# Clustered attention and a gated FFN on one core: one pair of heads turned by DMA in place of TensorE, and the next pair's turns put behind it

## The chip, the cores and the metric

The kernel runs on one core of a Trainium2 chip. The metric is the device time of one execution in microseconds (us); a lower one is better. The profiles are of single executions, taken by the hardware profiler.

## What is computed

Four batches of eight heads, 768 tokens, 64 numbers per head. Each query and key is assigned to one of 16 clusters (the centroid with the largest product); a query attends to the keys of its own cluster alone. The attention's result, heads side by side, goes through an FFN with a sigmoid gate.

```python
q_assign = argmax(q_n @ c_n.T); k_assign = argmax(k_n @ c_n.T)
mask   = q_assign[:, :, :, None] == k_assign[:, :, None, :]
scores = where(mask, scale * q @ k.T, -1e9)
attn   = softmax(scores)
x      = (attn @ v) as [4 * 768, 512]
out    = (sigmoid(x @ w_gate) * (x @ w_val)) @ w_out      # 512 -> 1536 -> 512
```

## The kernel before

**Heads as tiles.** For each head there is a tile `T` of 128 partitions by 12 blocks of 128 columns: six blocks of keys, six of queries, with the 64 numbers in partitions 0 to 63 and tokens along the columns. It comes from `hl`, the same with tokens in partitions: the numbers in f16 ("hi", a cast) and their rounding errors ("lo", a subtraction). Turning `hl` gives `T`. One group of 12 small matmuls per head then gives the cluster logits `lg`; VectorE takes their largest and writes one-hot rows `oh`, which are turned in their own right and laid over partitions 64 to 79 of `T` (in the queries as a large negative number where the cluster differs). One matmul of `T`'s keys against its queries then gives masked scores.

**Steps.** Everything runs to a clock of steps. A step is one scores matmul (line 1066: one block of keys against 384 queries), its exponential on ScalarE (line 1071), and the products of an earlier step with the values (line 1089). Batch 0 has steps 0 to 95, batch 1 steps 96 to 191, and so on. Pairs of heads are numbered 0 to 3; in batch 1 pair 0 is used from step 96 (its second head from 108), pair 1 from 120, pair 2 from 144. Between these, in each step, a queue of FFN work of the batch before is let out by a credit in nanoseconds: gate groups (`g`, line 532) and value groups (`v`, line 548) of four matmuls, then output products (`o`, line 865).

**The order of work** on each engine is the order in which the program emits it, and each engine works in order. What prepares a later pair is put at a step by a number in the table `SCHED`; half a step means ahead of the step's FFN work, a whole one behind it. The numbers `b1p1...` count from the step at which the pair is used; those of `g0...` and `g1...` are steps themselves.

**Two ways to prepare a pair.** `pieces` (batch 1's first `npe` pairs) turns on TensorE: six transposes at a time into a PSUM tile (line 1198), eviction by VectorE or ScalarE (lines 1211, 1209), the one-hot rows likewise (line 1250, then 1261 and 1263). Its steps are `hi`, `lo`, `tu`, `ev`, `lg`, `pk`, `ot`, `pl`. `pair_prep` (all other pairs of batches 1 to 3) turns by DMA from SyncE's queue: `sp` (cast on VectorE, line 1631, and subtraction on GpSimd, line 1632, for keys or queries of one head), `tn` (one DMA that turns a head, line 412), `lg` and `pk` (logits; their reading, the choice and the one-hot rows, lines 436, 451 to 471), `ot` (one DMA that turns a pair's one-hot rows, line 1649), `hp` (two small DMAs per head that carry them into `T`, line 492, here called hops).

```python
def turn(key, hl, pl):
    T[key] = pl.tile([128, hl.shape[1], 128], HP, tag="T", name="T")
    SP.dma_start_transpose(out=T[key], in_=hl.rearrange("p c x -> p (c x)"))
...
NPE = SCHED.get("npe", 1)
PEP = [(1, p) for p in range(NPE)]
...
for e in range(0 if (b, p) in PEP else 2):     # in pair_prep: nothing of a pair that pieces prepares
```

On SyncE's queue stand besides these the loads of later pairs (line 213), the stores of the result (line 504), and the turns of attention results `x` by DMA (line 1120; of batch 0's second half, those of pairs 1 and 2, at steps 74 and 87; the product that they wait for is GpSimd's, line 390). PSUM has four banks in a ring for scores, gates, values and logits, two for the value products, and two for outputs and for what TensorE transposes.

Of the kernel before, what the change touches and what calls it, by code (L numbers as in the profile page):

```python
# [19 lines left out]
]  # L20
SCHED = {
# [74 lines left out]
    "fwv": [354, 356, 357, 359, 364, 366, 370, 371], "b3p2pk1": -28.5, "END": 0,  # L96
}


# [1671 lines left out]
```

## Time and profile before

| | us |
|---|---|
| median of 3 runs | 318.93 (318.47 to 319.13) |
| the profiled execution | 319.12 |
| its span in the profile | 317.3 |
| TensorE busy | 310.0 |
| ScalarE busy | 244.9 |
| VectorE busy | 238.6 |
| GpSimd busy | 120.9 |

The span runs from the first instruction's start to the last one's end; what lies outside it is start and end of the program. A row of the timeline gives start, duration, engine, line, operation, what is written and read, and how many instructions it stands for. Matmuls overlap: a row's duration includes the tail of its last one, so the time that a group takes up is read from its start to the next row's start. For DMAs the duration is that of the issue on the queue; the landing is told apart.

### The profile page before, as it was taken

What the parts mean: (1) busy time and instruction counts of PE and PEld (TensorE: products, weight loads), DVE (VectorE), ACT (ScalarE), POOL (GpSimd) and SP (SyncE); (2) the same over time, 40 slices, a digit from 0 to 9 for tenths busy, and PEclk for the clock granted to TensorE, in tenths of its full rate; (3) what the DMA queues carried; (4) which work ended last, traced back from release to release, by engine and by line L of the source; (5) the groups of instructions that cost most, each with busy time, mean ns of one, the idle gap of its engine ahead of it and who ended that gap; (6) DMA issues with size and microseconds to landing.
All of it is one profiled execution on the core that took longest, in us unless ns stands there. A gap on an engine that the chain in (4) does not pass through costs nothing.

```text
span 317.3 us, 9228 instructions
## 1 busy us (share of the span) xinstructions
PE 310.0 (98%) x3492; PEld 218.8 (69%) x3492; DVE 238.6 (75%) x623; ACT 244.9 (77%) x555; POOL 120.9 (38%) x157
## 2 busy tenths in 40 slices
PE   7899999999999999999999999999999999999995
PEld 4688766766666666666777678766677678656685
DVE  5899756778688777686788688776888776678983
ACT  6688998797899887877776876777877887588621
POOL 5888454244434275423234333424212111026600
PEclk9999999999999999999999999999999999999999
DMA  7999998639848988976676455882506130300014
GB/s 196 379 259 169 271 164 143 176 83 264 242 100 163 204 221 136 199 217 161 106 193 153 151 118 134 248 153 53 112 2 76 55 27 14 145 1 3 0 35 165
DMA packets 77996, 45.16 MB, mean 142 GB/s; under 512 B 56896, under 2 KB 75520, under 8 KB 77952
## 3 DMA queue, kind: packets, MB, share of 16 engines
q1 hardware_dynamic: 73840, 39.66, 51.3%
q0 software_dynamic: 3680, 4.72, 9.1%
q8 instruction: 27, 0.44, 0.6%
q10 hardware_dynamic: 432, 0.20, 0.2%
q14 instruction: 17, 0.14, 0.1%
HBM read 28.34 MB, written 6.29 MB: 109 GB/s over the span
## 4 chain that ended last, share of the span: by engine, by line
PE 93%; DMA 2%; DVE 1%; POOL 1%; SPq 1%; issue 0%; ACT 0%; DVEq 0%
PE sc L1066 19%; PE g L532 15%; PE v L548 15%; PE av L1089 11%; PE o L994 9%; PE o L865 5%; PE lg L436 2%; PE o L699 2%; PE o_end L802 2%; PE av L699 2%; DMA kraw<-in_k_dram 2%; PE v L628 2%; PE y L699 2%; PE o L802 1%; PE av L802 1%; PE z L699 1%
## 5 line engine op out<-in xcount | busy, mean ns | idle before, releaser
L1071 ACT ACTIVATE es<-sc 128x384 f16<-128x384 f32 x384 | 174.1, 492 | 38.5 <-PE sc L1066 29.8
L1066 PE MATMUL sc<-T 128*128 128x384 f16 x384 | 117.3, 325 | 0.7 <-DVE T L1396 0.4
L1089 PEld LDWEIGHTS <-es 128*128 128x128 f16 x1152 | 81.3, 98 | 35.1 <-ACT es L1071 0.2
L1089 PE MATMUL av<-va,es 128*128 128x65 f16 x1152 | 97.6, 194 | 0.0
L553 DVE SCALAR_TENSOR_TENSOR hT<-th,v 128x384 f16<-128x384 f32 x72 | 39.8, 553 | 33.8 <-PE av L1089 29.6
L377 POOL TENSOR_TENSOR xp<-t,rec 128x384 f16<-128x384 f32 (+1 forms) x30 | 21.8, 726 | 97.3 <-DVE rec L374 49.2
L548 PE MATMUL v<-xTb,wv 128*128 128x384 f16 x288 | 58.5, 326 | 0.1
L532 PE MATMUL g<-xTb,wg 128*128 128x384 f16 x288 | 58.5, 326 | 0.0
L538 ACT ACTIVATE th<-g 128x384 f32<-128x384 f32 x72 | 35.4, 492 | 8.3 <-PE g L532 6.3
L1066 PEld LDWEIGHTS <-T 128*128 128x128 f16 x384 | 37.0, 96 | 1.2 <-DVE T L1396 0.7
L548 PEld LDWEIGHTS <-wv 128*128 128x128 f16 x288 | 28.0, 97 | 13.9 <-issue 0.3
L532 PEld LDWEIGHTS <-wg 128*128 128x128 f16 x288 | 27.9, 97 | 13.9
L1632 POOL TENSOR_TENSOR hl<-kraw,hl 128x384 f16<-128x384 f32 x22 | 20.2, 920 | 40.6 <-DVE hl L1631 25.9
L1632 POOL TENSOR_TENSOR hl<-qraw,hl 128x384 f16<-128x384 f32 x22 | 21.1, 961 | 11.1 <-DVE hl L1631 11.1
L865 PE MATMUL o<-wo,hT 128*128 128x512 f16 x72 | 19.9, 379 | 0.0
L372 DVE TENSOR_TENSOR t<-av,sv 128x390 f32<-128x390 f32 (+1 forms) x30 | 14.4, 480 | 7.1 <-PE av L1089 5.3
L941 DVE TENSOR_TENSOR ob<-o,ob 128x256 f32<-128x256 f32 (+1 forms) x28 | 15.0, 549 | 4.7 <-PE o L994 3.2
L708 POOL TENSOR_TENSOR hT<-T 128x384 f16<-128x384 f32 x12 | 11.8, 1001 | 16.2 <-DVE T L657 15.6
L994 PE MATMUL o<-wo,hT 128*128 128x256 f16 x108 | 16.8, 272 | 0.0
L994 PEld LDWEIGHTS <-sum 128*128 128x128 f16 x144 | 14.0, 97 | 3.3
L451 DVE TENSOR_REDUCE lgs<-lg 128x192 f32<-128x384 f32 x23 | 12.7, 551 | 3.0 <-PE lg L436 2.9
L324 POOL CAST va<-vraw 128x768 f16<-128x768 f32 x15 | 13.1, 873 | 2.4 <-DMA vraw<-in_v_dram 2.4
(225 smaller groups left out, 470.2 us busy)
## 6 DMA issues: line engine op xcount, KB each, us to landing
vraw<-in_v_dram SPq DMA_DIRECT2D x15, 384.0 KB, 4.9
kraw<-in_k_dram SPq DMA_DIRECT2D x14, 384.0 KB, 4.2
qraw<-in_q_dram SPq DMA_DIRECT2D x12, 384.0 KB, 4.1
out_dram<-ob SPq DMA_DIRECT2D x17, 256.0 KB, 2.2
wg<-in_moe_w_gate_dram POOLq DMA_DIRECT2D x2, 768.0 KB, 9.2
wv<-in_moe_w_val_dram POOLq DMA_DIRECT2D x2, 768.0 KB, 10.4
wo<-in_moe_w_out_dram POOLq DMA_DIRECT2D x2, 768.0 KB, 9.3
T<-ohT SPq DMA_DIRECT2D x44, 24.0 KB, 1.9
```

What stands on the lines that cost most here:

```text
L377: (eng or POOL).tensor_tensor(x, t[:, 0:nq, 0:64], bcast(rec[:, 0:nq], 64), ALU.mult)
L532: PE.matmul(out=g[:, 0:n], lhsT=wg[fc // WQ][:, dc, fc % WQ, :], rhs=xT[:, dc, t0 : t0 + n], start=(dc == 0), stop=(dc == NDC - 1),)
L538: ACT.activation(th[:, 0:n], g[:, 0:n], AF.Tanh)
L548: PE.matmul(out=w[:, 0:n], lhsT=wv[fc // WQ][:, dc, fc % WQ, :], rhs=xT[:, dc, t0 : t0 + n], start=(dc == 0), stop=(dc == NDC - 1),)
L553: DVE.scalar_tensor_tensor(HB[b, blk][:, fc, 0:n], st[0][:, 0:n], 1.0, w[:, 0:n], ALU.add, ALU.mult)
L699: PE.matmul(out=o, lhsT=l, rhs=r, start=start and d == 0, stop=stop and d == 1, skip_group_check=True,)
L865: PE.matmul(out=o, lhsT=HB[b, blk][:, fc, bass.ts(t, 128)], rhs=wo[fc // WON][:, fc % WON, :], start=(fc == 0), stop=(fc == NFC - 1),)
L994: PE.matmul(out=st[z][:, e], lhsT=a[:, c, :], rhs=rhs[:, c, :], start=start and c + e == 0, stop=c == HF - 1, skip_group_check=True,)
L1066: PE.matmul(out=sc.rearrange("p (c t) -> p c t", t=128), lhsT=s["k"], rhs=s["q"], start=True, stop=True,)
L1071: ACT.activation(es, sc, AF.Exp, scale=SCALE)
L1089: PE.matmul(out=av[:, a0 + s["c0"] + i, :], lhsT=s["es"][:, bass.ts(i, 128)], rhs=VA[b, p][:, e, s["j"], :], start=(first and i == 0 and a ...
L1632: POOL.tensor_tensor(hl[:, :, 64:128], r, hl[:, :, 0:64], ALU.subtract)
```

## The change

Three things are changed, all in the table `SCHED`. `npe` goes from 1 to 0, so that batch 1's pair 0 is prepared by `pair_prep` like the others: turned by two DMAs, its one-hot rows turned by a third and carried into `T` by four hops. Thirteen new numbers place its steps, counted from step 96 (`sp00` at -30 is step 66, `hp1` at -8 is step 88). And six numbers of pair 1, counted from step 120, are moved later: its casts and turns go from steps 60.5 to 79 to steps 71 to 80.

```diff
-    "halved1": 1, "halved0": 4, "npe": 1, ...
+    "halved1": 1, "halved0": 4, "npe": 0, ...
...
-    "b1p1sp00": -59.5, "b1p1sp01": -56.5, "b1p1tn0": -52, ...
-    "b1p1sp10": -48.5, "b1p1sp11": -46.5, "b1p1tn1": -41.0, ...
+    "b1p1sp00": -49, "b1p1sp01": -48, "b1p1tn0": -44, ...
+    "b1p1sp10": -45.5, "b1p1sp11": -44.5, "b1p1tn1": -40, ...
...
+    "b1p0sp00": -30, "b1p0sp01": -29, "b1p0sp10": -28, "b1p0sp11": -27,
+    "b1p0tn0": -25.5, "b1p0tn1": -23.5, "b1p0lg0": -17.5, "b1p0pk0": -16.5,
+    "b1p0lg1": -14.5, "b1p0pk1": -13.5, "b1p0ot": -12.5, "b1p0hp0": -8.5, "b1p0hp1": -8,
```

In steps, before and after:

| | before | after |
|---|---|---|
| pair 0, casts and subtractions | 68 to 85 | 66, 67 (head 0), 68, 69 (head 1) |
| pair 0, turns | 75.5, 78 (head 0), 84.5, 89.5 (head 1), on TensorE | 70.5, 72.5, by DMA |
| pair 0, logits | 79, 92 | 78.5, 81.5 |
| pair 0, one-hot rows turned | 82.5, 98.5, on TensorE | 83.5, by DMA |
| pair 0, one-hot rows placed | 83.5 to 104.5, by VectorE and ScalarE | 87.5, 88, by hops |
| pair 1, casts and subtractions | 60.5, 63.5, 71.5, 73.5 | 71, 72, 74.5, 75.5 |
| pair 1, turns by DMA | 68, 79 | 76, 80 |
| pair 1, logits | 81.5, 89 | 81.5, 89 |

More of the change, by code (lines that the diff above doesn't have):

```diff
@@ L95 @@
     "b3p0vs": -30, "b3p0vu": -28, "b3p0vt": -9, "b3p1lg0": -32, "b3p1pk0": -32, "fwg": [327, 327, 331, 331.5, 332, 341, 341, 344],
-    "fwv": [354, 356, 357, 359, 364, 366, 370, 371], "b3p2pk1": -28.5, "END": 0,
[1 row of a table added]
 }
```

7 rows, old and new, of the table SCHED are left out of this document.

## The prediction

> **What bounds the kernel now.** I read the page's busy times first, then its chain that ended last, then the busy times in the two stretches that the change touches.
>
> ```profile
> PE 310.0 (98%) x3492; PEld 218.8 (69%) x3492; DVE 238.6 (75%) x623; ACT 244.9 (77%) x555; POOL 120.9 (38%) x157
> ...
> PE 93%; DMA 2%; DVE 1%; POOL 1%; SPq 1%; issue 0%; ACT 0%; DVEq 0%
> ```
> ```profile
> 40.00:57.00 17.00, 17.00 (x177) 11.46 (x176) 10.74 (x28) 14.91 (x37) 9.28 (x12) 1.00 0.85 140
> 57.00:75.00 18.00, 18.00 (x217) 11.86 (x216) 13.14 (x35) 14.77 (x32) 5.11 (x7) 1.00 0.67 167
> ```
>
> The first pair of rows is the page's: TensorE (PE) is busy for 98% of the span and is 93% of the chain. The second pair gives stretch, length and busy time of PE, weight load, VectorE, ScalarE, GpSimd, then the granted clock (1.00), the DMA share and GB/s. PE is busy 17.00 of 17.00 us and 18.00 of 18.00 us, at full clock; VectorE has 6.3 us and 4.9 us to spare, GpSimd 7.7 us and 12.9 us, the DMA engines 15% and 33%. So a PE instruction taken out here is worth its slot, until PE has to wait for something; and a wait of PE costs its full length. I therefore read the PE timeline for the slots, and SyncE's (SP's) issues for the new waits.
>
> **What is removed.** Before, pair 0 of batch 1 is turned on PE, in four groups of six transposes for keys and queries (line 1198) and two of six for the one-hot rows (line 1250). Here are some groups, each with the row that follows it, and three logit groups and one score row that I use below:
>
> ```profile
> L1198 PE MATMUL t_ps<-identh,hl x24: 217/219/220, 55.2 to 68.2; 128*128 128x128 f16 x24
> ...
> L1250 PE MATMUL oh_ps<-identh,oh x12: 218/219/219, 61.7 to 75.5; 128*128 128x128 f16 x12
> ```
> ```profile
> 55.19 0.50 PE L1198 MATMUL t_ps<-identh,hl 128*128 128x128 f16 x6
> 55.52 0.81 PE L548 MATMUL v<-xTb,wv 128*128 128x384 f16 x4
> ...
> 58.83 0.45 PE L436 MATMUL lg<-cm,T 128*128 128x32 f16 x12
> 59.13 0.32 PE L1066 MATMUL sc<-T 128*128 128x384 f16 x1
> ...
> 61.10 0.45 PE L436 MATMUL lg<-cm,T 128*128 128x32 f16 x12
> 61.40 0.25 PE L1089 MATMUL av<-va,es 128*128 128x65 f16 x3
> ...
> 61.65 0.50 PE L1250 MATMUL oh_ps<-identh,oh 128*128 128x128 f16 x6
> 61.99 0.81 PE L532 MATMUL g<-xTb,wg 128*128 128x384 f16 x4
> ...
> 62.92 0.81 PE L548 MATMUL v<-xTb,wv 128*128 128x384 f16 x4
> 63.56 0.26 PE L1089 MATMUL av<-va,es 128*128 128x65 f16 x3
> 63.66 0.33 PE L1066 MATMUL sc<-T 128*128 128x384 f16 x1
> ...
> 67.44 0.45 PE L436 MATMUL lg<-cm,T 128*128 128x32 f16 x12
> ...
> 73.36 0.32 PE L1066 MATMUL sc<-T 128*128 128x384 f16 x1
> ```
>
> The 0.50 us of a group includes the tail of its last matmul; the slot is from its start to the next start: 55.52 - 55.19 = 0.33 us and 61.99 - 61.65 = 0.34 us, so 0.335 us for six, 56 ns each. Six groups are 6 x 0.335 = **2.0 us** of PE time, the whole possible gain. The logit groups (12 matmuls, 59.13 - 58.83 = 0.30 us each) stay two in number and only change place: head 0's stays at step 79, head 1's moves up from step 92 to just before pair 1's at step 82 (the row at 61.10).
>
> One rule speaks against taking this work off PE. The Trainium skill, "VectorE: DVE Perf Modes", sections "The three transpose paths" and "Rules for kernel authors", says to transpose 128x128 on TensorE where PSUM will do as destination and gives 390 ns for a block there against 1309 ns by DMA. By its figure, as an estimate, 36 blocks off PE would be 14 us; the slots above, in a stream that is never idle, say 2.0 us, and no run here shows a block in isolation. What the DMA path does here is worked out below from this trace's landings.
>
> Gone from ScalarE and VectorE are four evictions and four copies of one-hot rows, and VectorE gets two more casts and two small multiplications. Neither engine ends a wait of PE in these stretches, so I cost this at nothing: the cover is the idle time above, and GpSimd's extra subtractions (four in place of two and a cast) fit its 7.7 us.
>
> **What is added: DMA work on SP, and waits of PE for it.** These are SP's issues before, and for some of them the time from issue to landing (the view of DMA issues, cut to one issue at a time, in the order of the text).
>
> ```profile
> 50.19 1.44 SPq L412 DMA_TRANSPOSE T<-hl  x1
> 56.33 1.18 SPq L1120 DMA_TRANSPOSE xTb<-xp  x1
> 57.57 0.57 SPq L213 DMA_DIRECT2D kraw<-in_k_dram  x1
> 58.19 0.46 SPq L213 DMA_DIRECT2D vraw<-in_v_dram  x1
> 58.70 0.47 SPq L213 DMA_DIRECT2D qraw<-in_q_dram  x1
> 59.33 2.42 SPq L412 DMA_TRANSPOSE T<-hl  x1
> 67.91 1.18 SPq L1120 DMA_TRANSPOSE xTb<-xp  x1
> ...
> 72.22 1.21 SPq L1649 DMA_TRANSPOSE ohT<-oh  x1
> ...
> 77.37 2.50 SPq L492 DMA_DIRECT2D T<-ohT  x4
> ```
> ```profile
> T<-hl SPq DMA_TRANSPOSE x1, 3.3
> ```
> ```profile
> T<-hl SPq DMA_TRANSPOSE x1, 6.2
> ```
> ```profile
> ohT<-oh SPq DMA_TRANSPOSE x1, 5.1
> ```
> ```profile
> T<-ohT SPq DMA_DIRECT2D x1, 24.0 KB, 2.0
> ```
>
> (50.19, 59.33, 72.22, and the second of the four that begin at 77.37: at 0.6 us each it is issued at about 78.0.) The row at 50.19 is pair 1's first head (step 68), 59.33 its second (step 79). SP works in order, and so do the landings on its queue: 59.33 took 6.2 us because three loads of 384 KB went ahead. After, the order on SP is: pair 0's head 0 (step 70.5), its head 1 (72.5), the x turn of 56.33 (74), pair 1's head 0 (76), the three loads, pair 1's head 1 (80), pair 0's one-hot turn (83.5), the x turn of 67.91 (87), pair 0's four hops (87.5, 88). Everything that PE waits for there:
>
> ```profile
> 48.32 0.82 POOL L324 CAST va<-vraw 128x768 f16<-128x768 f32 x1
> 53.26 0.96 POOL L1632 TENSOR_TENSOR hl<-kraw,hl 128x384 f16<-128x384 f32 x1 [4.12 <-DVE hl L1631]
> 54.18 0.91 POOL L1632 TENSOR_TENSOR hl<-qraw,hl 128x384 f16<-128x384 f32 x1
> 55.48 0.82 POOL L390 TENSOR_TENSOR xp<-t,rec 128x384 f16<-128x384 f32 x1 [0.39 <-DVE rec L389]
> ```
>
> 1. Pair 0's turns. GpSimd's subtractions follow the cast of 48.32 and come 0.9 us apart, so two are ready at about 50.1 and four at 51.9 us. Head 0 is turned at 50.2 and lands 3.3 later, at 53.5; head 1 at 52.0 lands at 55.3. PE reads head 0 no earlier than 58.83 - 0.67 - 0.81 = 57.3 us (two groups gone, and a value group of 0.81 us that went ahead of it now behind it), head 1 at 61.10 - 0.67 = 60.4. Cover 3.8 and 5.1 us: no cost. Pair 1's first two subtractions end at about 53.7, ahead of the x product at 55.48, so the x turn stays at 56.33.
>
> 2. Pair 1's head 0 now stands behind that x turn: issue at 57.57, as kraw before, landing 3.3 later at 60.8 to 60.9. PE wants it at 61.10 - 0.67 + 0.30 (head 1's group ahead of it) = 60.7. Its cover was 61.10 - 53.5 = 7.6 us and is now nothing: a wait of 0.1 to 0.3 us.
>
> 3. Pair 1's head 1 stands behind the three loads, all later by one turn's issue, 1.44 us. Before it landed at 59.33 + 6.2 = 65.5; if it is later by that, 67.0; if the loads only close up behind the turn ahead of them, 66.2 (an estimate: half the delay). PE wants it at 67.44 - 4 x 0.335 + 0.30 = 66.4, or 66.6 with the wait of point 2: 0 to 0.4 us.
>
> 4. Two logit groups now lie side by side, in two of the four PSUM banks that scores, gates and values share, until VectorE has read both. One reading and choice takes
>
> ```profile
> 62.77 0.56 DVE L451 TENSOR_REDUCE lgs<-lg 128x192 f32<-128x384 f32 x1
> 63.36 0.35 DVE L462 TENSOR_REDUCE mx<-lgs 128x12 f32<-128x192 f32 x1
> 63.75 0.43 DVE L464 TENSOR_TENSOR oh<-lgs,mx 128x96 f16<-128x96 f32 x2
> 64.21 0.19 DVE L471 TENSOR_SCALAR oh<-oh 128x96 f16<-128x96 f16 x1
> ```
>
> that is 1.6 us; the first starts at about 61.0, so the second bank is read at 61.0 + 1.6 + 0.55 = 63.1. PE needs that bank again four or five allocations on, at the value group of 62.92 or the scores of 63.66, which after stand 0.67 + 0.34 - 0.30 = 0.7 us earlier and point 2's wait later, at 62.4 or 63.1: a wait of 0.7 us or of nothing. I take a quarter of a microsecond, since the wait of point 2 moves PE towards it.
>
> 5. Pair 0's hops, before head 0's scores at step 96 (73.36). One-hot turn at about 63.1 (SP is in the turn of point 3 until then). Before, from the one-hot turn's issue to the landing of the first head's second hop took 78.0 + 2.0 - 72.22 = 7.8 us; so 70.9. PE comes to step 96 at 73.36 - 5 x 0.335 = 71.7 plus the waits above. Cover 0.8 us or more: no cost.
>
> Sum: 2.0 - 0.2 - 0.15 - 0.25 = **1.4 us** gained. Nothing gives it back later: PE is the bound on both sides of these stretches. The profiled execution took 319.12 us (span 317.3 and 1.8 around it), so 317.7 for its like; it lies 0.2 us above the median of the runs, 318.93, so the forecast is **317.5 us**. With no waits it is 316.9; with all at their upper ends (0.3 + 0.4 + 0.7) it is 318.3.
>
> **The rivals.** A measurement of this kernel tells about 0.2%, 0.6 us, from no change.
>
> *The DMA queue eats the gain* (about the same time). The turn of point 3 grows: SP's descriptors back up one transfer earlier, its issue comes a microsecond later and it lands at 68.0 to 68.5; PE waits 1.5 us there, and 0.3 us before it: 318.7. For: the 2.42 us issue at 59.33, against 1.44 elsewhere, shows SP already held back behind three loads. Against: DMA engines are 33% idle there. Chance 0.15.
>
> *Head 0's one-hot rows come too late* (slower). On the DMA path the way from logits to placed rows crosses SP's queue twice, behind other transfers. It decides where the first head's second hop lands after 71.7 + 2.0 = 73.7 with no other wait, 10.6 us after the one-hot turn's issue; every microsecond beyond is lost. With a one-hot turn held 2 us by late choices on VectorE and a hop 2 us late behind the x turn of 67.91 (in front of the hops on SP), it lands at 75: 318.93 - 2.0 + 3.3 = 320.2. Against it: 7.8 us in the rows. Chance 0.13. The rule of the Trainium skill's page "VectorE: DVE Perf Modes" that is cited above would have this outcome, since it prefers TensorE wherever PSUM will do; the trace speaks for it only in the landing times, 3.3 to 6.2 us a turn.
>
> *The full 2.0 us* (no wait binds): 316.9. Part of the forecast's case below.
>
> **How the numbers follow.** Forecast case, gains from 0.7 to 2.0: 0.72. Queue case 0.15, slower case 0.13. Faster by over 0.2% takes the forecast case alone, 0.72; within 0.2% the queue case, 0.15; slower 0.13. The forecast's own range is 316.9 to 318.3. For 8 in 10 it takes in part of the queue case, up to 318.9, and 0.2 us of measurement below: 316.7 to 318.9.
>
> **What would show it.** Right: no groups at lines 1198 and 1250, PE 36 instructions fewer, turns from line 412 at 24 in place of 22 and hops at 48 in place of 44, with the first two turns near 50 and 52 us; small idle time of PE before logit groups around 60.5 and 66.5 us, under a microsecond in sum, and none at step 96; step 120 earlier by 1.2 to 2.0 us, and the end by as much. Wrong: a PE idle of over a microsecond before a logit group (queue case), or before the scores of step 96 released by the hops (slower case); a gain that is there at step 120 and gone at the end; or ends of waits on VectorE in many small pieces, which would mean that its slack was not there.

## The result

The changed kernel is slower: 320.76 us median (320.56 to 321.57) against 319.0 us for the kernel before, a ratio of 1.005 with a 95% interval of 1.0027 to 1.0074. Run again later with more executions the ratio was 1.0033 (1.0011 to 1.0055). The forecast was 317.5 us, between 316.7 and 318.9.

The profiled execution after took 321.57 us, with a span of 319.8 us; it is the slowest of the first four executions. Of its page, the busy times and the chain that ended last:

```profile
PE 309.1 (97%) x3456; PEld 217.3 (68%) x3456; DVE 238.4 (75%) x621; ACT 241.6 (76%) x550; POOL 122.3 (38%) x158
...
PE 82%; DMA 8%; DVE 4%; POOL 2%; issue 1%; ACT 1%; SPq 1%; DVEq 0%; POOLq 0%; ACTq 0%
```

TensorE has the 36 instructions fewer, but its share of the chain fell from 93% to 82%, and DMA and VectorE have taken that over. The view of waits, TensorE from 40 us on, names nobody before. After, it has three rows (who waited for whom, us in total, times, longest; `hT`, line 553, is the FFN's hidden product, which frees the PSUM bank of a value group):

```profile
PE lg L436 <- DMA T<-hl: 1.8, 2, 1.0
PE v L548 <- DVE oh L464: 1.0, 1, 1.0
PE lg L436 <- DVE hT L553: 0.5, 1, 0.5
```

On the timeline of TensorE these waits stand at four places, steps 79, 111, 116 and 130; the brackets give the idle time ahead and its releaser:

```profile
56.73 0.33 PE L1066 MATMUL sc<-T 128*128 128x384 f16 x1
57.59 0.28 PE L436 MATMUL lg<-cm,T 128*128 128x32 f16 x5 [0.53 <-DVE hT L553]
...
82.72 0.34 PE L548 MATMUL v<-xTb,wv 128*128 128x384 f16 x1 [1.01 <-DVE oh L464]
87.06 0.29 PE L436 MATMUL lg<-cm,T 128*128 128x32 f16 x5 [0.86 <-DMA T<-hl]
96.10 0.27 PE L436 MATMUL lg<-cm,T 128*128 128x32 f16 x4 [0.99 <-DMA T<-hl]
```

An idle time leaves out the tail of the matmul ahead. Measured from start to start, with the usual slot of the instruction ahead taken off, the four are 0.69, 1.17, 1.02 and 1.16 us; four smaller ones between steps 82 and 95 come to 0.76 and one at step 187 to 0.31. These nine sum to 5.1 us. Against the 2.0 us saved that makes 3.1 us lost. The scores rows of the two timelines come to 2.9: the lead-in, all that runs ahead of the change, happened to be 0.52 us shorter in the execution after, and from that

| step | start before | start after | after against before, lead-in taken off |
|---|---|---|---|
| 75 | 54.12 | 53.60 | 0.00 |
| 96 | 73.36 | 72.56 | -0.28 |
| 111 | 82.55 | 81.39 | -0.64 |
| 117 | 86.33 | 87.38 | +1.57 |
| 132 | 95.23 | 97.31 | +2.60 |
| 192 | 128.36 | 130.76 | +2.92 |
| 381 | 267.34 | 269.74 | +2.92 |

So there are two losses. Up to step 111 a gain of 2.0 us came to 0.64. Then, behind everything that the change adds, 3.6 us are lost, and afterwards nothing more. (The other three executions are 0.8 to 1.0 us shorter than the profiled one. A second profile, told below, lost less, and in part elsewhere.)

What stands behind the second loss is on SyncE's queue. First some rows of before: pair 2's two turns and pair 3's first (line 412), between them the loads of keys for pair 3 (73.49) and for a later pair (81.94). Then the queue after, from pair 0's one-hot turn on:

```profile
69.27 1.39 SPq L412 DMA_TRANSPOSE T<-hl  x1
...
73.49 0.57 SPq L213 DMA_DIRECT2D kraw<-in_k_dram  x1
...
79.92 1.35 SPq L412 DMA_TRANSPOSE T<-hl  x1
...
81.94 0.44 SPq L213 DMA_DIRECT2D kraw<-in_k_dram  x1
...
87.26 1.42 SPq L412 DMA_TRANSPOSE T<-hl  x1
```
```profile
62.92 2.54 SPq L1649 DMA_TRANSPOSE ohT<-oh  x1
66.96 1.18 SPq L1120 DMA_TRANSPOSE xTb<-xp  x1
69.88 2.49 SPq L492 DMA_DIRECT2D T<-ohT  x4
72.48 1.43 SPq L412 DMA_TRANSPOSE T<-hl  x1
...
75.11 1.23 SPq L1649 DMA_TRANSPOSE ohT<-oh  x1
76.39 0.57 SPq L213 DMA_DIRECT2D kraw<-in_k_dram  x1
...
80.80 2.44 SPq L492 DMA_DIRECT2D T<-ohT  x4
83.68 1.42 SPq L412 DMA_TRANSPOSE T<-hl  x1
...
85.78 0.44 SPq L213 DMA_DIRECT2D kraw<-in_k_dram  x1
...
87.47 3.95 SPq L412 DMA_TRANSPOSE T<-hl  x1
```

Pair 2's first turn goes from 69.27 to 72.48, its second from 79.92 to 83.68, the loads from 73.49 to 76.39 and from 81.94 to 85.78. The row of SyncE's waits between 60 and 100 us for hops that wait for a one-hot turn, before and then after:

```profile
SPq L492 <- DMA ohT<-oh: 0.6, 1, 0.6
```
```profile
SPq L492 <- DMA ohT<-oh: 4.5, 2, 2.8
```

Twice, after, the hops stood at the head of the queue until a one-hot turn had landed, 4.5 us in all. The turn issued at 62.92 took

```profile
ohT<-oh SPq DMA_TRANSPOSE x1, 6.9
```

6.9 us, behind three loads and pair 1's second turn. So the hops began at 69.88, 1.7 us after the queue's entry ahead of them had been issued (66.96 + 1.18), and took 2.6 us to issue; what stands behind them was 3 to 4 us later than before. Pair 2's second turn landed 3.3 us after its issue, at 87.0, and TensorE waited for it at step 116. Before, it had landed at 83.1 and was wanted at 86.0 (the logits; below them the landing of the turn of 79.92, in us):

```profile
86.02 0.46 PE L436 MATMUL lg<-cm,T 128*128 128x32 f16 x12
```
```profile
T<-hl SPq DMA_TRANSPOSE x1, 3.2
```

Pair 3's first turn was issued hardly later than before (87.47, before 87.26), but now right behind three loads that had come 3.8 us later. It landed 8.6 us after its issue, at 96.05, where before it took 3.2 us, and TensorE waited at step 130. At step 111 the wait comes through VectorE:

```profile
81.58 0.36 DVE L1631 CAST hl<-kraw 128x384 f16<-128x384 f32 x1 [3.08 <-DMA kraw<-in_k_dram]
```

a cast for pair 3 stood still for 3.1 us until its keys (the load of 76.39) had landed, ahead of the choice for pair 2 that frees a PSUM bank.

### The profile page after: what moved, and what is told of

The parts are those of the page before. It is cut to its first block, busy times and chain, and to the rows that moved or that the text cites. A ratio compares the mean times of both kernels' runs of the same rounds, so it can differ in the third digit from the quotient of the medians.

```text
span 319.8 us, 9172 instructions
## 1 busy us (share of the span) xinstructions
PE 309.1 (97%) x3456; PEld 217.3 (68%) x3456; DVE 238.4 (75%) x621; ACT 241.6 (76%) x550; POOL 122.3 (38%) x158
## 4 chain that ended last, share of the span: by engine, by line
PE 82%; DMA 8%; DVE 4%; POOL 2%; issue 1%; ACT 1%; SPq 1%; DVEq 0%; POOLq 0%; ACTq 0%
PE sc L1066 16%; PE v L548 14%; PE g L532 13%; PE av L1089 9%; PE o L994 9%; DMA T<-hl 5%; DMA kraw<-in_k_dram 3%; PE o L865 3%; PE o L699 2%; PE lg L436 2%; PE o_end L802 2%; PE av L699 2%; PE y L699 2%; PE v L628 2%; PE av L802 1%
## 5 line engine op out<-in xcount | busy, mean ns | idle before, releaser
L1089 PEld LDWEIGHTS <-es 128*128 128x128 f16 x1152 | 81.5, 98 | 35.0 <-ACT es L1071 0.2
L548 PE MATMUL v<-xTb,wv 128*128 128x384 f16 x288 | 58.5, 326 | 1.1 <-DVE oh L464 1.0
L532 PE MATMUL g<-xTb,wg 128*128 128x384 f16 x288 | 58.5, 326 | 0.0
L1632 POOL TENSOR_TENSOR hl<-kraw,hl 128x384 f16<-128x384 f32 x24 | 22.1, 921 | 35.5 <-DVE hl L1631 19.6
L1632 POOL TENSOR_TENSOR hl<-qraw,hl 128x384 f16<-128x384 f32 x24 | 22.9, 955 | 12.0 <-DVE hl L1631 11.4
```

What stands on the lines that cost most here:

```text
L532: PE.matmul(out=g[:, 0:n], lhsT=wg[fc // WQ][:, dc, fc % WQ, :], rhs=xT[:, dc, t0 : t0 + n], start=(dc == 0), stop=(dc == NDC - 1),)
L548: PE.matmul(out=w[:, 0:n], lhsT=wv[fc // WQ][:, dc, fc % WQ, :], rhs=xT[:, dc, t0 : t0 + n], start=(dc == 0), stop=(dc == NDC - 1),)
L1089: PE.matmul(out=av[:, a0 + s["c0"] + i, :], lhsT=s["es"][:, bass.ts(i, 128)], rhs=VA[b, p][:, e, s["j"], :], start=(first and i == 0 and a ...
L1632: POOL.tensor_tensor(hl[:, :, 64:128], r, hl[:, :, 0:64], ALU.subtract)
```

## The experiments

The theory with which I began: the place and the waits on SyncE's queue decide (queue order). Rivals: the added bytes (DMA traffic), and casts and choices that crowd each other on VectorE and GpSimd. All ratios are to the kernel before, run beside each on the same chip (medians 318.9 to 319.1 us), with 95% intervals. A ratio is an estimate over all executions and not the quotient of two medians, from which it differs by up to 0.0017 here.

**Hops behind pair 2's first turn.**

```diff
-    "b1p0hp0": -8.5, "b1p0hp1": -8,
+    "b1p0hp0": -4.9, "b1p0hp1": -4.9,
```

> The changed kernel with pair 0's four hops put behind pair 2's first turn on SyncE's queue (step 91.1 in place of 87.5 and 88). Queue-order theory: the hops, which wait on the queue until the one-hot turn has landed at 69.8 us, hold up everything behind them by some 3 us, and TensorE's waits of about 1 us each at steps 111, 116 and 130 come of that. With the turn ahead of the hops (issued near 68 us in place of 72.5) the queue runs 1.4 us earlier from there, and each of the three waits shrinks by about that much, to 0 to 0.2 us: 318.0 to 318.8. DMA-traffic theory (two more turns of 384 KB make all transfers later, whatever their order): no change, 320.5 to 321. VectorE/GpSimd theory (casts and choices that crowd each other are the main loss): the 1.5 us of waits at steps 79 to 95 stay, and so does the time, 320 to 321.

Measured: 319.39 us, 1.0006 (0.999 to 1.0022). Pair 2's turn was issued at 69.3 in place of 72.5, and TensorE's waits at steps 116 and 130 are gone (the rows below are steps 96, 111 and 79):

```profile
PE sc L1066 <- DMA T<-ohT: 0.6, 1, 0.6
PE v L548 <- DVE oh L464: 0.6, 1, 0.6
PE lg L436 <- DVE hT L553: 0.5, 1, 0.5
```

The same work in another order gives back 0.9 us against the ratio 1.0033 of the changed kernel, 1.4 us against 1.005; DMA traffic would not, though against 1.0033 the intervals overlap. It did not reach the 318.0 to 318.8 expected, since the hops now land too late for step 96 (0.6) and step 111 keeps 0.6.

**One-hot rows on TensorE, turns by DMA.**

```diff
+    if (b, p) == (1, 0):  # in ot()
+        st["ot"] = turns(NCH * 128, name="oh_ps")
+        for c in range(NCH):
+            PE.transpose(st["ot"][:, bass.ts(c, 128)], st["oh"][:, c, :], identh)
+        return
...
+    if (b, p) == (1, 0):  # in hops(e)
+        for s in range(2):
+            r = 64 * e + 32 * s
+            DVE.tensor_copy(
+                T[b, e][64:80, 6 * s : 6 * s + 6, :].rearrange("p c t -> p (c t)"),
+                st["ot"][r : r + 16, :],
+            )
+        return
```

> The changed kernel with pair 0's one-hot rows of both heads turned by six TensorE transposes and placed by four copies of VectorE: the one-hot turn and the four hops are gone from SyncE's queue, the two turns by DMA stay. Queue-order theory: from 63 us on the queue is as in the kernel before, the waits at steps 111, 116 and 130 are gone, the early ones (about 1.2 us) stay, five groups of transposes are saved: 319.0 - 1.7 + 1.2 = 318.5. DMA-traffic theory: the one-hot turn and the hops are 0.3 MB of the 1.1 MB added, so most of the late waits stay: 320 or more.

Measured: 318.76 us, 0.9987 (0.9971 to 1.0003). In the view of waits none after step 96 is left; 0.5 and 0.3 us remain, both before it and both on VectorE. The two added turns of heads are there, 0.8 of the 1.1 MB added, so their bytes are not what costs.

**Pair 1 back at its old steps; only pair 0 changed.**

```diff
-    "b1p1sp00": -49, "b1p1sp01": -48, "b1p1tn0": -44,
+    "b1p1sp00": -59.5, "b1p1sp01": -56.5, "b1p1tn0": -52,
-    "b1p1sp10": -45.5, "b1p1sp11": -44.5, "b1p1tn1": -40,
+    "b1p1sp10": -48.5, "b1p1sp11": -46.5, "b1p1tn1": -41.0,
```

> The changed kernel with pair 1's casts and turns at their old steps (60.5 to 79), so pair 0 alone is changed. Queue-order theory: pair 1's first turn is issued before the loads again, so the loads, pair 1's second turn and pair 0's one-hot turn all come 1.4 us earlier, the hops are issued near 68.4 in place of 69.9, and the late waits shrink from about 1 us to 0 to 0.3 each: about 318.5. DMA-traffic theory: the same bytes, so 320.5 or more.

Measured: 318.73 us, 0.9971 (0.995 to 0.9993): faster than the kernel before. Of the whole list of waits one is left:

```profile
PE v L548 <- DVE oh L464: 0.6, 1, 0.6
```

So pair 0's part is a gain, if a small one (the medians alone, 318.73 against 319.12, give 0.9988; two later runs below bear it out), and the move of pair 1 turns it into a loss. The bytes are the same, which leaves nothing to the DMA-traffic theory. The hops now began at 67.60 without the wait of 1.7 us.

**An idle one-hot turn and four idle hops in the kernel before.**

```diff
+    at(83.5, lambda: SP.dma_start_transpose(out=zt[:, 0:6], in_=wg[0][:, 0].rearrange("p q f -> p (q f)")))
+    at(87.5, lambda: [hop(zt, s, zT, 6 * s, 6) for s in range(2)])
+    at(88, lambda: [hop(zt, 2 + s, zT[32:], 6 * s, 6) for s in range(2)])
```

> The kernel before with an idle one-hot turn (128 x 768 f16, of weights, at step 83.5) and four idle hops (steps 87.5 and 88) put on SyncE's queue; they write memory that is not used at that time, and nothing waits for them. Queue-order theory: the queue behind them gets some 2.5 to 3 us later from 69 us on, as in the changed kernel, and TensorE waits at steps 111 to 130 by up to 1 us each: 320.5 to 322. DMA-traffic theory: 0.3 MB more changes little: 319.0 to 319.4.

Measured: 318.69 us, 0.9987 (0.9972 to 1.0003). My expectation failed. The queue did get later, but nothing at steps 111 to 130 waited; the one wait of this profile, 1.1 us, is far behind, at step 177, for another pair's turn:

```profile
69.04 2.50 SPq L492 DMA_DIRECT2D kheld<-vheld  x4
71.70 1.42 SPq L412 DMA_TRANSPOSE T<-hl  x1
...
82.17 1.47 SPq L412 DMA_TRANSPOSE T<-hl  x1
```

Pair 2's turns stand at 71.70 and 82.17, 2.4 and 2.3 us later than before, and their cover of 2.9 us (86.0 against 83.1) takes that. The time that the new entries hold the queue is not enough by itself; in the changed kernel the lateness is 3.2 and 3.8 us, which is 3.7 and 4.3 with the lead-in taken off, and by that count TensorE comes 0.6 us earlier at step 111.

**Pair 1 late, pair 0 on TensorE.** The same six numbers, put into the kernel before.

```diff
-    "b1p1sp00": -59.5, "b1p1sp01": -56.5, "b1p1tn0": -52,
+    "b1p1sp00": -49, "b1p1sp01": -48, "b1p1tn0": -44,
-    "b1p1sp10": -48.5, "b1p1sp11": -46.5, "b1p1tn1": -41.0,
+    "b1p1sp10": -45.5, "b1p1sp11": -44.5, "b1p1tn1": -40,
```

> The kernel before with only pair 1's casts and turns moved to steps 71 to 80; pair 0 stays on TensorE. Queue-order theory: the loads and pair 1's second turn come 1.4 us later on the queue, no one-hot turn and no hops of pair 0 follow, so the cover of 3 to 4 us behind them holds: TensorE waits at most 0.7 us, all before step 96, 319.0 to 319.7. If pair 1's move itself were the main loss: 320 or more.

Measured: 321.44 us, 1.0068 (1.0049 to 1.0087), outside both. The trace has one wait, and it is none of those in the changed kernel:

```profile
PE t_ps L1198 <- POOL hl L1178: 1.9, 1, 1.9
```

Pair 1's subtractions stood on GpSimd ahead of pair 0's own, which TensorE's transposes needed. So this run says nothing of the move's price in the changed kernel; it shows that the old place of pair 1's casts had been needed by pair 0's old way of turning.

**One cast of pair 1 later.**

```diff
-    "b1p1sp11": -44.5,
+    "b1p1sp11": -43,
```

> The changed kernel with one cast of pair 1 (its second head's queries) put at step 77 in place of 75.5, behind a hidden-unit product of VectorE instead of ahead of it. The wait of 0.7 us before the logits of step 79 should go. If the waits of the changed kernel add up one by one, the time falls by that, to 320.0. If the queue sets the time (pair 2's second turn lands near 87.0 and pair 3's first near 96.0 whenever TensorE comes), TensorE only arrives sooner and waits longer there: 320.7, no change.

Measured: 320.14 us, 1.0032 (1.0016 to 1.0048), beside 1.005 and 1.0033 for the changed kernel: not told apart. The wait at step 79 went, and others came for it:

```profile
PE lg L436 <- DMA T<-hl: 1.4, 4, 0.6
PE v L548 <- DVE oh L464: 0.9, 1, 0.9
PE sc L1066 <- DMA T<-ohT: 0.2, 1, 0.2
```

Two of the four in the first row are at steps 82 and 89: TensorE now reached pair 1's logits before pair 1's turns had landed. So in this profile the early gain was held from two sides, by VectorE and by those landings.

**Pair 3's first cast later.**

```diff
-    "b1p3sp00": -60.5,
+    "b1p3sp00": -58.5,
```

> The changed kernel with the first cast of pair 3 at step 109.5 in place of 107.5, so that VectorE's choice for pair 2 (step 108.5) no longer stands behind a cast that waits for keys still on their way (a 3.1 us idle time of VectorE). The 1.0 to 1.2 us wait of TensorE at step 111 should go. If the waits add up one by one: 319.6. If the queue sets the time: the wait comes back before the logits of steps 116 and 130, 320.7.

Measured: 320.84 us (319.06 to 322.37), 1.0045 (1.0024 to 1.0065). No gain, as the queue-order theory has it, but not by its path: in the profiled execution (319.59 us) the waits at steps 111, 116 and 130 were all absent and one of 1.0 us stood at step 89 for pair 1's second turn, which took 7.6 us to land. The executions of this one kernel differ by up to 3.3 us, so one profile does not settle where the time of the median goes.

**Three edits together**: pair 1 back, pair 3's first cast at -58.5, and pair 0's second logits apart from pair 1's.

```diff
-    "b1p0lg1": -14.5, "b1p0pk1": -13.5, "b1p0ot": -12.5,
+    "b1p0lg1": -16, "b1p0pk1": -15, "b1p0ot": -14,
```

> The changed kernel with three edits: pair 1's casts and turns at their old steps, pair 0's second logits at step 80 (choice 81, one-hot turn 82) so that two logit groups no longer lie side by side, and pair 3's first cast at step 109.5. The run with pair 1's old steps alone took 0.997 of the kernel before, with 0.8 us of waits at step 111 and 0.5 us at steps 82 to 87 left. Queue-order theory with cover left on the queue: most of these 1.3 us are gained, 317.2 to 317.8, 0.993 to 0.996 of the kernel before. If the queue sets the time there too, the waits return later: 318.5.

Measured: 318.6 us, 0.9985 (0.9974 to 0.9996), no better than pair 1 back alone. The wait at step 111 is gone, but from step 73 to 118 many of 0.1 to 0.3 us stand before TensorE, on hidden products and exponentials, 1.7 us in all. No gain is seen from spreading the logits.

**The changed kernel once more, and three variants beside it on one chip.**

> The changed kernel once more, on the same chip as the three variants and with more executions: 1.004 to 1.007 of the kernel before. The late waits (steps 111 to 130) should differ between executions by up to a microsecond with the landing of pair 1's one-hot turn (80.7 us in the first profile; 78.8 us in the run with pair 3's cast later), and the waits at steps 79 to 95 (1.2 to 1.6 us) should not.

Measured: 320.41 us (318.96 to 321.48), 1.0033 (1.0011 to 1.0055), below the 1.004 to 1.007 expected. In this profiled execution (320.30 us, close to the median) pair 1's second turn took 7.9 us to land and TensorE waited 1.3 us for it at step 89. Step 111 waited 0.6 us, steps 116 and 130 for nothing; I had expected the early waits to stay the same.

```profile
68.79 0.27 PE L436 MATMUL lg<-cm,T 128*128 128x32 f16 x4 [1.27 <-DMA T<-hl]
```

Pair 1's first head alone put back (first and second line of that diff):

> The changed kernel with only pair 1's first head put back (casts at steps 60.5 and 63.5, turn at 68); its second head stays at 74.5, 75.5 and 80. So the loads go 1.4 us earlier on SyncE's queue, as with the whole pair put back (0.997 of the kernel before), but the second head's casts stay crowded. If the place in the queue is what pair 1's move cost: 0.996 to 0.999 of the kernel before, and no wait for pair 1's turns at steps 82 and 89. If the crowd of casts and subtractions is: 1.001 to 1.003.

Measured: 318.42 us, 0.9991 (0.9973 to 1.0009). No turn is waited for any more. The wait on VectorE at step 79 (first row) is still there, and one is left at step 111 (second row):

```profile
PE lg L436 <- DVE hT L553: 0.5, 1, 0.5
PE v L548 <- DVE oh L464: 0.3, 1, 0.3
```

Issuing this one turn early again, and not just ahead of the loads, recovers 0.4% of the time beside it on the same chip. The edit moves that head's two casts as well, but the wait on VectorE at step 79 stays, so most of what pair 1's move cost is its place on the queue. What is left against pair 1 wholly back (0.9991 beside 0.9976 in the next run) is within the intervals; that it comes from the crowded casts is not shown.

Pair 1 back and pair 3's first cast later:

> The changed kernel with pair 1 at its old steps and pair 3's first cast at step 109.5 in place of 107.5; the logits stay side by side. Against the run with pair 1's old steps alone (0.997, with a wait of 0.8 us at step 111 behind a cast that waits for a load): that wait goes and 0.4 to 0.6 us of waits at steps 73 to 87 stay: 0.994 to 0.996, 317.3 to 317.9. If the queue brings the wait back at steps 116 to 130: 0.997.

Measured: 318.2 us, 0.9976 (0.9959 to 0.9993). The wait at step 111 is gone from its profile; the ratio is about that of pair 1 back alone, 0.9971, and the gain expected is not seen.

Pair 1 back and the one-hot rows on TensorE:

> The changed kernel with pair 1 at its old steps and pair 0's one-hot rows turned by six TensorE transposes and placed by VectorE: the two turns by DMA alone are left of the change. Five groups are saved (1.7 us), no hops, nothing of pair 0 on the queue after 55 us. Queue-order theory: nothing late from step 96 on, only VectorE's part of the early waits (0.5 to 1.0 us): 317.9 to 318.5, 0.996 to 0.998. DMA-traffic theory would want it slower than the kernel before, as the turns' 0.8 MB are all there.

Measured: 317.82 us (317.24 to 319.18), 0.9967 (0.9952 to 0.9982): the fastest median, and faster than both kernels. Nothing of pair 0 is on the queue after its two turns, and only two small waits are left:

```profile
PE oh_ps L1651 <- DVE oh L471: 0.3, 1, 0.3
PE g L628 <- DMA xTb<-xp: 0.2, 1, 0.2
```

Five groups of transposes are saved here. Four go to the two DMA turns; the fifth, 0.34 us of the 1.7, is saved because one group now turns the one-hot rows of both heads, which has nothing to do with DMA.

Set side by side, four of these ratios tell what the loss takes:

| | one-hot rows by DMA and hops | one-hot rows on TensorE |
|---|---|---|
| pair 1 late, as in the change | 1.005 and 1.0033 | 0.9987 |
| pair 1 at its old steps | 0.9971 | 0.9967 |

Either part alone leaves no loss. The loss of some 2 us needs both: pair 1's first turn in the place where the loads were issued before, which makes all behind it later, and pair 0's one-hot turn and hops behind the loads.

## Why the prediction was wrong

**The 2.0 us of transposes: right.** 3492 to 3456 instructions, and the table of steps closes only with that saving.

**Point 1, pair 0's turns: right in the verdict.** The second was issued at 52.7, since subtractions waited for casts, and landed at 56.4 us, still well ahead of the logits at 60.6.

**Points 2 and 3, pair 1's turns: the mechanism right, the second one's size too small.** The first landed at 60.5 as reckoned (57.34 + 3.2). The second was bounded at 5.4 to 6.2 us from its issue (66.2 and 67.0 less 60.8); it took 6.3 in the first profile, 7.9 in the second. With 66.9 us, step 89's logits could not come earlier than before (67.44 less the shorter lead-in): whatever was saved up to there was lost again. In the first profile that shows as waits on VectorE, with one cast later as waits for the turns. In the second profile the turn landed at 68.7 us and TensorE waited 1.3 us for it, where point 3 had 0 to 0.4. This is what the queue rival (chance 0.15) described: landing at 68.0 to 68.5 and a wait of 1.5 us. Its time, 318.7, has none of the losses behind step 96.

**VectorE and GpSimd "at nothing": wrong.** I took the idle time, 6.3 us in 17, for cover, and left open how long a cast takes. Where a cast met a subtraction it took longer:

```profile
56.01 1.07 DVE L1631 CAST hl<-qraw 128x384 f16<-128x384 f32 x1
56.99 0.54 DVE L553 SCALAR_TENSOR_TENSOR hT<-th,v 128x384 f16<-128x384 f32 x1
...
55.93 0.92 POOL L1632 TENSOR_TENSOR hl<-kraw,hl 128x384 f16<-128x384 f32 x1
```

The cast of 56.01 ended 0.2 us after the subtraction that ran beside it. At 1.07 us it took three times what a cast takes alone (0.32 to 0.36 us, the 33 of this trace that met no GpSimd instruction), and the hidden product behind it freed its PSUM bank 0.7 us late for the logits of step 79. It is no single case: of the 15 casts of the trace that began beside a GpSimd instruction, 12 took 0.37 to 1.07 us and ended 0.22 us after it; the other three took 0.35. The Trainium skill, "SBUF — State Buffer", section "SBUF: two separate sides", says that GpSimd shares one pair of ports with VectorE, which needs it in a two-port mode or with two inputs in SBUF, that whichever starts first holds it for its whole instruction, and that the other is blocked until then. The 12 casts agree; in which mode they ran, no run here shows. An average idle share is no cover for an instruction with someone waiting behind it.

**Point 4, logits side by side: the size.** I took 0.25 us; steps 82 to 87 lost 0.53. The trace names hidden products of VectorE (steps 82 and 87) and ScalarE's `th` (84) as what ended these waits, and not the reading of the logits themselves. Setting the logits apart did not give it back.

**Point 5, the hops: wrong, and here the main step failed.** I asked only whether they land before step 96. I reckoned 70.9 us from the row of the kernel before, 7.8 us after the one-hot turn's issue; it was 72.4, 9.5 after it, and step 96 waited 0.23 us. That much was nearly right. What I left out is who stands behind the hops on SyncE: their wait for the one-hot turn (1.7 us) and their issue (2.6 us) made pair 2's turns, the loads and the second set of hops 3 to 4 us late. Pair 3's first turn, behind such loads, landed 5.5 us later than before. In the first profile steps 111, 116 and 130 paid 3.4 us for it, in the second step 111 alone 0.7. "Nothing gives it back later" was argued from TensorE being the bound, while the covers of 2.9 us behind it were never looked up.

**The slower rival** (chance 0.13) had the chain of hops and a time, 320.2, close to the measured one, but its price at step 96. The slowdown came one pair later, from the same queue, so the closeness is luck.

What stays open: why the landing of the same turn differs between executions (6.3 and 7.9 us), and with it which of the waits an execution has. It is not the change alone: in the run with idle entries the turn, at its old step, took 8.1 us, and nobody waited. The three long landings (7.6, 7.9 and 8.1 us) are all in runs with a one-hot turn issued right behind it, but seven other such runs have 5.8 to 6.3. So how the loss divides between step 89 (point 3) and the steps behind 96 (point 5) is open as well: of the two, the first profile has it all behind 96, while the second, whose execution is closer to the median, has more at step 89. For both holds what the experiments show: the term of the sum that failed is the price of the added entries on SyncE's queue, put at 0.35 us for pair 1's turns and at nothing for pair 0's hops. Taking either off its late place brings the ratio from 1.0033 or 1.005 to 0.9971 or 0.9987. The intervals are over executions, so the comparisons hold; each ledger of waits is that of one execution.

## What to carry to other kernels

When a step is moved onto a DMA queue that issues in order, as SyncE's does here, go through every later entry of that queue until it is idle, and set its new landing against the time at which it is wanted; the covers there (2.9 us here) are what the change may use up. An entry that waits for data at the head of a queue makes everyone behind it later. And two moves may each be harmless and cost time together: here the DMA turns, with the next pair left where it was and the one-hot rows kept on TensorE, are 0.3% faster than before, while the whole is 0.3 to 0.5% slower.

## What the runs showed of the hardware

A VectorE cast of 0.35 us takes up to 1.07 us when a GpSimd subtraction of 0.92 us began just ahead of it; 12 casts of the trace that were stretched ended 0.22 us after the GpSimd instruction beside them. A DMA turn of a head lands 3.2 us after its issue where no load stands right ahead of it on the queue (the turns of 57.34 and 72.48), and 6.3 and 8.6 us after it right behind three loads of 384 KB (60.55 and 87.47); a one-hot turn behind such a turn took 6.9 us (62.92).
